# Chunk (0, 8): from reciprocals copied between partition groups by GpSimd to a VectorE mask and four identity matmuls

## The chip, the cores and the metric

One core of a Trainium2 chip runs the whole program in one launch. Five engines work side by side, each through its own queue in order: TensorE (PE in the profile, with its weight loads shown apart as PEld), VectorE (DVE), ScalarE (ACT), GpSimd (POOL) and SyncE (SP), which here only issues DMAs. The metric is the device time of the program in microseconds. Three runs of the kernel before gave a median of 184.01 us (183.97 to 184.29).

## The reference

Four batches of four heads, 1088 tokens, head dimension 32. A polynomial sketch of q and k, a linear attention over it, and then a feed-forward layer with a squared ReLU on all 4352 tokens:

```python
def phi(x):                      # x: [b, h, s, 32]; S1, S2: [8, 32]
    a = np.einsum('rd,bhsd->bhsr', S1, x)
    b = np.einsum('rd,bhsd->bhsr', S2, x)
    return np.einsum('bhsi,bhsj->bhsij', a, b).reshape(*x.shape[:-1], 64)
kv = np.einsum('bhsf,bhsd->bhfd', phi(k), v)
z = np.sum(phi(k), axis=2)
num = np.einsum('bhsf,bhfd->bhsd', phi(q), kv)
den = np.einsum('bhsf,bhf->bhs', phi(q), z)[..., None] + 1e-06
x = (num / den), heads side by side, as [4352, 128]
h = np.maximum(x @ w_in, 0.0)    # 128 -> 2048
out = h * h @ w_out              # 2048 -> 128
```

## The kernel before

**Two halves that overlap.** The attention makes `xT`, the transposed input of the feed-forward layer, in chunks. Batch 0 has three: 256 tokens made by a prologue of its own, then chunk (0, 8) and chunk (0, 20), which begin at group 8 and group 20 of 32 tokens and hold 12 and 16 groups (`nb`). The batches after have one chunk each. The feed-forward layer goes over `xT` in ten column chunks `FC` of 256, 384, 448, 448, 512, 512, 512, 512, 512 and 256 columns. Each column chunk has 16 slices of the hidden dimension, put into units of one or two slices. Per unit, TensorE runs `mm1` (line 600, into a PSUM tile `pg`), ScalarE or VectorE takes the ReLU (lines 612 and 610) and the square (lines 623 and 625), and TensorE runs `mm2` (line 644), which accumulates all 16 slices in one PSUM bank, the tile `po`. Column chunk 0 has 256 columns and units 0 to 8, so its `po` uses columns 0 to 255 of its bank. Column chunk 1 has 384 columns, units 9 to 24, and reads just the 384 tokens that chunk (0, 8) writes into `xT`.

**The steps of an attention chunk**, for chunk (0, 8), in their order:

- `qT`: VectorE transposes q; `qc` (line 306): TensorE sketches it with 32-row, 32-column tiles of its array.
- `qt` (485), `pd` (491), `rc` (501 and 505): VectorE transposes back, multiplies, sums and takes reciprocals. They stand in `rc` with a partition group (32 partitions) for each token share c and columns for each head h.
- `rl` (513): sixteen GpSimd copies, four for each c, move them to `rd`, where a partition group belongs to a head. `rl` c = 0, 1 serve the first half of the chunk, c = 2, 3 the second.
- `qb`, `qa0`, `qa1` (522), `qp` (537): six VectorE shuffles and four products make the sketch's outer products.
- `nd` (553): TensorE multiplies them with `kv`, again on 32x32 tiles, into the PSUM tile ring `att`.
- `bc` x = 0, 1 (563): VectorE broadcasts a half of `rd` along 32 columns by a transpose; `x` (570): VectorE multiplies `nd` by it and writes `xT`.

**The order of the work** is not written out. A class `_Order` is given every task with an engine, a duration, a key (its due time) and what it needs. It plays them through with durations given in the code: an engine that is free takes the ready task with the lowest key; a task that needs another engine's result is ready a `hop` of 0.25 after its end, and `lag` later still where one is given. VectorE also holds back for a task with a lower key that gets ready within half of the chosen task's duration. The instructions are then emitted in the order of the planned starts, and each engine runs its own in that order. The feed-forward matmuls have a fixed sequence among themselves; around unit 4 it is: mm2 of units 3 and 4 with mm1 of units 7 and 8 behind them, then mm2 of units 5 and 6, mm1 of unit 9, mm2 of unit 7, mm1 of unit 10. Tasks such as `qc` and `nd` are put between these as they get ready. The framework adds the semaphores between engines from the tiles that instructions read and write.

**Other names.** `iden` is the 128x128 identity, `irep` (line 730) holds a 32x32 identity in every partition group and column group, and `own_h` is [128, 4], 1 where a partition belongs to partition group h. `x0` is a PSUM tile of the prologue: TensorE writes its columns 384 to 391 (line 836), ScalarE reads these (line 840), TensorE then writes columns 256 to 383 (line 443).

Of the kernel before, what the change touches and what calls it, by code (L numbers as in the profile page):

```python
# [9 lines left out]
F32 = mybir.dt.float32  # L10
# [4 lines left out]
def _ap(t: bass.AP, p0: int, np_: int, off: int, free):  # L15
    p = list(t.ap)[0]
    return bass.AP(
        t.tensor, t.offset + p0 * p[0] + off, [[p[0], np_]] + [list(d) for d in free]
    )
# [88 lines left out]
def kernel(  # L108
# [11 lines left out]
    nc = tc.nc  # L120

    B, H, S, D = 4, 4, 1088, 32
# [6 lines left out]
    LU = 4  # L129
    KC = [(0, 160), (160, 128)]  # L130
    W0, W1, W3 = 8, 0, 1
    ND, QT, WI, KL, QL = 2, 6.0, (1.0, 1.9), (30.0, 8.0), 4.0

# [9 lines left out]
    mult = mybir.AluOpType.mult  # L145
# [8 lines left out]
    wpool = ctx.enter_context(tc.tile_pool(name="work", bufs=2))  # L154
# [5 lines left out]
    def sb(name, cols, dt=F32, rows=128):  # L160
        return cpool.tile([rows, cols], dt, tag=name, name=name)
# [90 lines left out]
    for i in range(2):  # L252
        nc.vector.memset(own_p[64 * i : 64 * i + 64, i : i + 1], 1.0)
    iden, irep = sb("iden", 128), sb("irep", 128)
# [3 lines left out]
    own_h, own_q = sb("own_h", 4), sb("own_q", 2)  # L258
# [7 lines left out]
        out=own_h[:, :], in_=_ap(iden, 0, 128, 0, [[32, 4], [1, 32]]), op=add, axis=AX  # L266
# [3 lines left out]
        out=own_f[:, :], in_=_ap(iden, 0, 128, 0, [[8, 16], [1, 8]]), op=add, axis=AX  # L270
# [6 lines left out]
    st = {}  # L277
# [4 lines left out]
    def banks(t_, x, col, n, k=2):  # L282

        return _ap(t_, 0, 128, 512 * x + col, [[512, k], [1, n]])
# [223 lines left out]
    def a_rl(b, i0, nb, c):  # L508
        n = nb // 4
        if c == 0:  # L510
            st[b, "rd", i0] = wpool.tile([128, 4 * NT], F32, tag="rd", name="rd")
        for h in range(H):
            nc.gpsimd.tensor_copy(  # L513
                st[b, "rd", i0][32 * h : 32 * h + 32, n * c : n * c + n],
                st["rc"][32 * c : 32 * c + 32, n * h : n * h + n],
            )

    def a_qs(b, i0, nb, which, x):
# [60 lines left out]
    for ci, (c0, n) in enumerate(FC):  # L579
        first_unit[c0] = len(units)  # L580
        nb = 512 // n
# [153 lines left out]
    for w in sw:  # L735
# [3 lines left out]
        out=_ap(sfk, 0, 128, 0, [[16, 2], [1, 16]]),  # L739
        in0=_ap(ss, 0, 128, 64, [[0, 2], [1, 16]]),  # L740
        in1=_ap(own_q, 0, 128, 0, [[1, 2], [0, 16]]),
        op=mult,
# [35 lines left out]
    for t0, n in ((0, 2), (2, 2), (4, 3), (7, 2)):  # L778
# [6 lines left out]
        out=_ap(qp0, 0, 128, 0, [[256, 2], [1, 256]]), in0=banks(x0, 2, 0, 256),  # L785
        in1=_ap(qb0, 0, 128, 0, [[256, 2], [1, 256]]), op=mult,
    )
    den0 = psf.tile([128, 512], F32, tag="po", name="den0")
    for y in range(2):
        nc.tensor.matmul(  # L790
            den0[64 * y : 64 * y + 64, 0:128], eps[0:1, 0:64], eps[0:1, 64:192],
            start=True, stop=False,
# [4 lines left out]
    for c in range(4):  # L797
        cast_wi(c)
    nc.vector.tensor_tensor(
        out=_ap(zb, 0, 128, 1, [[65, 2], [32, 2], [1, 1]]),  # L800
        in0=_ap(st[0, "kvp"], 0, 128, 32, [[64, 2], [0, 2], [1, 1]]),
        in1=_ap(own_p, 0, 128, 0, [[0, 2], [1, 2], [1, 1]]),
        op=mult,
    )
    nc.vector.tensor_tensor(
        out=_ap(bd, 0, 128, 0, [[64, 2], [32, 2], [1, 32]]),
        in0=_ap(st[0, "kvp"], 0, 128, 0, [[64, 2], [0, 2], [1, 32]]),
        in1=own, op=mult,
    )
    nc.vector.tensor_tensor(  # L810
        out=_ap(zm, 0, 128, 0, [[16, 2], [8, 2], [1, 8]]),
        in0=_ap(st[0, "kvp"], 0, 128, 32, [[64, 2], [0, 2], [1, 8]]),
        in1=_ap(own_f, 0, 128, 0, [[0, 2], [8, 2], [1, 8]]),
        op=mult,
# [20 lines left out]
    for h in range(H):  # L835
        nc.tensor.matmul(
            x0[32 * h : 32 * h + 32, 384:392], s2f[:, :], zm[:, 8 * h : 8 * h + 8],
            skip_group_check=True,
# [5 lines left out]
    for _ in range(W3):  # L844
# [10 lines left out]
        out=xT[:, 0:256], in0=num0[:, 0:256], in1=bc0[:, :], op=mult  # L855
# [4 lines left out]
    O = _Order()  # L860
# [11 lines left out]
    def dve(n):  # L872
        return 0.067 + n / 960
# [4 lines left out]
    def on(f, *args):  # L878
        return lambda eng: f(*args)
# [4 lines left out]
    def glued(name, dur_, to, emit, uses=[]):  # L884
        O.add(name, {"PE": dur_}, -1000.0, [to], emit, uses=uses)
        O.by_name[name]["users"] = O.by_name[to]["users"]

    def q_tasks(b, i0, nb, key):

        m = 16 * nb  # L890
        k0 = key - 6.0 - 8 * dve(m)
        names = []
        for x in range(0 if (b, i0) == (0, 8) else 2):
            i1, n1 = i0 + x * (nb // 2), nb // 2
            n1 = min(n1, G - i1)
            names.append(("qT", b, i1))
            O.add(
                names[-1], {"DVE": dve(32 * n1)}, k0 - 1.5,
                ([("qn", b)] if b else []) + prev["qTuse"], on(a_qT, b, i1, n1),
                at=QT if i0 == 20 else 0.0,  # L900
            )
        kb = KB.get((b, i0))
        O.add(
            ("qc", b, i0), {"PE": 0.75}, k0 - 1.0,
            names + [("w", b)] + ([("kT", kb, 0), ("kT", kb, 18)] if kb else []),
            on(a_qc, b, i0, nb), rings=[("att", 1)], lag=PEL, at=0.4,
        )
        if kb:
            glued(("kc", kb), 0.65, ("qc", b, i0), lambda eng: a_kc(kb, st[b, "qc", i0]))
        prev["qTuse"] = [("qc", b, i0)] if i0 + nb == 4 * NT else []  # L910
        for x in range(2):
            O.add(
                ("qt", b, i0, x), {"DVE": dve(m)}, k0 - 0.3 + 0.1 * x, [], on(a_qt, b, i0, nb, x),
                uses=[("qc", b, i0)], rings=[("qt", 1)] if x == 0 else [],
            )
        more = 0.2 if (b, i0) == (0, 8) else 0.0
        rc = [("rc", b, j) for j, _ in AC[b] if j < i0] or [("rc", b - 1, j) for j, _ in AC[b - 1]]
        O.add(
            ("pd", b, i0), {"DVE": dve(8 * nb) + more}, k0 - 0.1, rc, on(a_pd, nb),
            uses=[("qt", b, i0, 0), ("qt", b, i0, 1)],  # L920
        )
        O.add(
            ("rc", b, i0), {"DVE": 0.2 + 0.65 * more + nb * 17 / 960}, k0 - 0.1, [], on(a_rc, nb),
            uses=[("pd", b, i0)], rings=[("rc", 1)],
        )
        for c in range(4):
            O.add(
                ("rl", b, i0, c), {"POOL": 0.8 + 1.25 * more}, k0 + 0.1 * c, [], on(a_rl, b, i0, nb, c),
                uses=[("rc", b, i0)], rings=[("rd", 2)] if c == 0 else [],
            )  # L930
        for w_ in ("qb", "qa0", "qa1"):
            for x in range(2):
                O.add(
                    (w_, b, i0, x), {"DVE": dve(m)}, k0, [], on(a_qs, b, i0, nb, w_, x),
                    uses=[("qc", b, i0)], rings=[(w_, 1)] if x == 0 else [],
                )
                k0 += 0.1
        for e in range(E):
            for x in range(2):
                O.add(  # L940
                    ("qp", b, i0, e, x), {"DVE": dve(m)}, k0 + 2.0, [], on(a_qp, b, i0, nb, e, x),
                    uses=[(f"qa{e}", b, i0, x), ("qb", b, i0, x)],
                    rings=[("qp", 3), ("qp", 3)] if (e, x) == (0, 0) else [],
                )
                k0 += 0.1

    def nd_tasks(b, i0, nb, key):
        m = 16 * nb
        qps = [("qp", b, i0, e, x) for e in range(E) for x in range(2)]
        kb, vb = NK.get((b, i0)), NV.get((b, i0))  # L950

        O.add(
            ("nd", b, i0), {"PE": 0.6 + 1.05 * max(nb, 14) / 36}, key - 3.5 - 4 * dve(m),
            [("kvr", b, h) for h in range(H)]
            + ([("kT", kb, 0), ("kT", kb, 18)] if kb else [])
            + ([("vn", vb), ("ks", vb, 3)] if vb else []),
            on(a_nd, b, i0, nb, (0,) if kb or vb else (0, 1)), uses=qps + [("qp", b, i0, 0, 0)], rings=[("att", 1)], lag=PEL,
        )
        if kb:
            def behind(eng):  # L960
                a_kc(kb, st[b, "nd", i0], start=False)
                a_nd(b, i0, nb, (1,))

            glued(("kc", kb), 0.65, ("nd", b, i0), behind)
        if vb:
            def behind(eng):
                a_kvs(vb, st[b, "nd", i0], 32 * NT, start=False)
                a_nd(b, i0, nb, (1,))

            glued(  # L970
                ("kvs", vb), 1.25, ("nd", b, i0), behind, [("kp", vb, h) for h in range(H)],
            )
        for x in range(2):
            O.add(
                ("bc", b, i0, x), {"DVE": dve(m)}, key - 2.5 - 4 * dve(m) + 0.1 * x, [], on(a_bc, b, i0, nb, x),
                uses=[("rl", b, i0, 2 * x), ("rl", b, i0, 2 * x + 1)],
                rings=[("bc", 1)] if x == 0 else [],
            )
            O.add(
                ("x", b, i0, x), {"DVE": dve(m)}, key - 2.0 - 4 * dve(m) + 0.1 * x, [], on(a_x, b, i0, nb, x),  # L980
                uses=[("bc", b, i0, x), ("nd", b, i0)]
                + ([("kc", kb)] if kb else []) + ([("kvs", vb)] if vb else []),
            )
# [93 lines left out]
    for u in range(NU):  # L1077
# [40 lines left out]
        if d0 + m == NB and ci != last:  # L1118
            po = [x for u_ in range(first_unit[c0], u + 1) for x in pe2[u_]]
# [4 lines left out]
                uses=[("oT", c0)],  # L1124
# [47 lines left out]
```

## Time and profile before

| what | value |
|---|---|
| median of three runs | 184.01 us |
| time of the profiled execution | 183.99 us |
| its span (first to last instruction) | 182.1 us |
| TensorE busy | 177.3 us (97%) |
| VectorE busy | 122.1 us (67%) |
| ScalarE busy | 136.6 us (75%) |
| GpSimd busy | 39.1 us (21%) |
| granted TensorE clock | 0.998 |
| GpSimd copies of line 513, 80 in all | 19.6 us |
| of these, the 16 of chunk (0, 8) | 15.74 to 20.07 us |

The span is what the trace shows of the program's instructions; 1.9 us of the time lie outside it. Busy times overlap, so they do not add up. A matmul in float32 stands in the trace as two weight loads and two matmul records; the matmuls of `mm1`, in float32r, as one. Matmul ends are modelled and neighbours overlap in the pipeline, so the time that one costs is read from the distance to the one before it, not from its own length. The chain of waits gives this distance directly.

### The profile page before, as it was taken

The numbers are of one execution on the slowest core, as the hardware profiler recorded it, in microseconds if no ns is written. First come the engines' busy times: TensorE is split into PE (matmuls) and PEld (weight loads), VectorE is DVE, ScalarE is ACT, GpSimd is POOL, SyncE is SP. The second block draws the span as 40 slices with busy tenths as digits, with TensorE's granted clock in tenths as the row PEclk, the third lists the DMA queues.
The fourth block names the chain that finished last, engine by engine and source line by source line (L and its number), as shares of the span: only waits on it lengthen the run. The fifth ranks groups of instructions, "written<-read, shape, count | busy, mean of one in ns | idle before, by whom it ended". The sixth has DMA issues, their size and how long they took to land.

```text
span 182.1 us, 3998 instructions
## 1 busy us (share of the span) xinstructions
PE 177.3 (97%) x1530; PEld 104.6 (57%) x1530; DVE 122.1 (67%) x262; ACT 136.6 (75%) x259; POOL 39.1 (21%) x158
## 2 busy tenths in 40 slices
PE   8999999999999999999999999999999999999992
PEld 2768776656555655655555554545554555555792
DVE  5979879999999951899994335996353334333640
ACT  3449679759947886799937778995777777777980
POOL 3545318348200003470018000600000000000000
PEclk9999999999999999999999999999999999999999
DMA  5799993010029700000031200003003000300211
GB/s 174 196 274 337 246 257 96 7 29 0 0 47 243 175 0 4 4 2 0 0 54 24 34 0 5 0 0 59 0 4 58 0 0 6 51 0 0 35 26 29
DMA packets 26146, 11.26 MB, mean 62 GB/s; under 512 B 17936, under 2 KB 25104, under 8 KB 26128
## 3 DMA queue, kind: packets, MB, share of 16 engines
q1 hardware_dynamic: 25936, 10.95, 24.8%
q8 instruction: 12, 0.20, 0.4%
q10 hardware_dynamic: 192, 0.07, 0.1%
q14 instruction: 6, 0.05, 0.1%
HBM read 8.78 MB, written 2.23 MB: 60 GB/s over the span
## 4 chain that ended last, share of the span: by engine, by line
PE 93%; DMA 2%; DVE 2%; SPq 0%; issue 0%; ACT 0%; ACTq 0%
PE po L644 61%; PE pg L600 18%; PE nd L553 3%; DMA qn<-in_q_dram 2%; PE po L639 2%; PE pol L639 2%; PE qc L306 1%; PE nd L417 1%; PE kvp L399 1%; PE qc L350 1%; PE kvp L417 1%; DVE kp L334 1%; SPq L181 0%; DVE g L625 0%; PE nd L350 0%; PE den L826 0%
## 5 line engine op out<-in xcount | busy, mean ns | idle before, releaser
L644 PE MATMUL po<-g,w_o 128*128 128x512 f32 (+3 forms) x288 | 122.7, 547 | 0.2 <-DVE g L625 0.2
L612 ACT ACTIVATE gt<-pg 128x512 f32<-128x512 f32 (+3 forms) x144 | 75.3, 570 | 31.4 <-PE pg L600 30.9
L644 PEld LDWEIGHTS po<-g,w_o 128*128 128x128 f32 x288 | 53.4, 189 | 32.3 <-issue 24.6
L600 PE MATMUL pg<-xT,w_in 128*128 128x512 f32 (+3 forms) x160 | 70.2, 520 | 0.0
L623 ACT ACTIVATE g<-gt 128x512 f32<-128x512 f32 (+2 forms) x102 | 60.7, 623 | 1.6
L625 DVE TENSOR_TENSOR g<-gt 128x512 f32<-128x512 f32 (+3 forms) x43 | 30.4, 708 | 39.5 <-ACT gt L612 38.8
L600 PEld LDWEIGHTS pg<-xT,w_in 128*128 128x128 f32 x160 | 29.2, 190 | 28.3 <-ACT gt L612 11.5
L513 POOL COPY rd<-rc 32x9 f32<-32x9 f32 (+2 forms) x80 | 19.6, 246 | 25.8 <-DVE rc L505 22.6
L459 POOL COPY kv<-kvt 32x64 f32<-32x64 f32 x48 | 12.7, 265 | 44.6 <-DVE kvt L436 42.5
L522 DVE STREAM_SHUFFLE qa<-qc 128x576 f32<-128x576 f32 (+2 forms) x20 | 11.8, 648 | 0.0
L537 DVE TENSOR_TENSOR qp<-qa,qb 128x576 f32<-128x576 f32 (+2 forms) x20 | 10.8, 604 | 0.0
L485 DVE STREAM_TRANSPOSE qt<-qc 128x576 f32<-128x576 f32 (+2 forms) x10 | 5.8, 608 | 6.2 <-PE qc L350 4.5
L370 DVE TENSOR_TENSOR kp<-fs 128x576 f32<-128x576 f32 x12 | 8.7, 741 | 0.0
L648 DVE STREAM_TRANSPOSE oT<-po 128x512 f32<-128x512 f32 (+3 forms) x9 | 5.9, 654 | 2.1 <-PE po L644 2.1
L553 PE MATMUL nd<-qp,kv 32*32 32x288 f32 (+2 forms) x320 | 6.6, 354 | 0.0
L522 DVE STREAM_SHUFFLE qb<-qc 128x576 f32<-128x576 f32 (+2 forms) x10 | 6.1, 651 | 0.0
L570 DVE TENSOR_TENSOR xT<-nd,bc 128x576 fp32r<-128x576 f32 (+2 forms) x10 | 5.6, 592 | 0.5 <-PE nd L553 0.5
L299 DVE STREAM_TRANSPOSE qT<-qn 128x192 f32<-128x192 f32 (+3 forms) x11 | 5.8, 554 | 0.2 <-DMA qn<-in_q_dram 0.2
L639 PE MATMUL po<-w_o,g 128*128 128x128 f32 x32 | 5.8, 280 | 0.0
L639 PE MATMUL pol<-w_o,g 128*128 128x128 f32 x32 | 5.7, 275 | 0.0
L563 DVE STREAM_TRANSPOSE bc<-rd 128x576 f32<-128x576 f32 (+2 forms) x10 | 5.7, 598 | 0.0
L553 PEld LDWEIGHTS nd<-qp,kv 32*32 32x32 f32 x320 | 2.9, 103 | 3.6 <-issue 2.4
(106 smaller groups left out, 89.2 us busy)
## 6 DMA issues: line engine op xcount, KB each, us to landing
kn<-in_k_dram SPq DMA_DIRECT2D x3, 544.0 KB, 7.2
qn<-in_q_dram SPq DMA_DIRECT2D x3, 544.0 KB, 7.8
vn<-in_v_dram SPq DMA_DIRECT2D x9, 144.0 KB, 6.0
w_in<-in_moe_w_in_dram SPq DMA_DIRECT2D x4, 256.0 KB, 4.2
w_o<-in_moe_w_out_dram SPq DMA_DIRECT2D x4, 256.0 KB, 5.1
out_dram<-oT SPq DMA_DIRECT2D x12, 64.0 KB, 1.9
out_dram<-oT SPq DMA_DIRECT2D x8, 56.0 KB, 1.9
out_dram<-oT SPq DMA_DIRECT2D x8, 48.0 KB, 1.8
```

The lines of the kernel that those rows point to most:

```text
L370: nc.vector.tensor_tensor(out=_ap(st[b, "kp"], 0, 128, 64 * NT * h, [[64, NT], [8, 8], [1, 8]]), in0=_ap(fs, 0, 128, o, [[32, NT], [1, 8], ...
L459: nc.gpsimd.tensor_copy(_ap(st[b, "kv"], 32 * c, 32, 64 * h, [[32, E], [1, 32]]), _ap(st["kvt"], 32 * h, 32, 0, [[64, E], [1, 32]]),)
L513: nc.gpsimd.tensor_copy(st[b, "rd", i0][32 * h : 32 * h + 32, n * c : n * c + n], st["rc"][32 * c : 32 * c + 32, n * h : n * h + n],)
L522: nc.vector.stream_shuffle(in_=banks(st[b, "qc", i0], 2 * x, 0, m), out=_ap(st[b, which, i0], 0, 128, 2 * m * x, [[m, 2], [1, m]]), mask=m ...
L537: nc.vector.tensor_tensor(out=st[b, "qp", i0, e][:, r], in0=st[b, f"qa{e}", i0][:, r], in1=st[b, "qb", i0][:, r], op=mult,)
L553: nc.tensor.matmul(nd[32 * h : 32 * h + 32, 512 * c : 512 * c + m], kv[r, o : o + 32], qp[r, m * h : m * h + m], start=(e == 0), stop=(e = ...
L600: nc.tensor.matmul(st["pg", u][:, n * i : n * i + n], w_in[:, 128 * (d0 + i) : 128 * (d0 + i) + 128], xT[:, c0 : c0 + n],)
L612: nc.scalar.activation(gt[:, 0:w], st["pg", u][:, 0:w], Relu)
L623: nc.scalar.activation(to, of, Square)
L625: nc.vector.tensor_tensor(out=to, in0=of, in1=of, op=mult)
L639: nc.tensor.matmul(po[x // 128][:, 0:128], g[:, x : x + 128], w, start=(d == 0), stop=(d == NB - 1),)
L644: nc.tensor.matmul(po[0][:, 0:n], w, g, start=(d == 0), stop=(d == NB - 1))
```

## The change

For chunk (0, 8) alone, `rd` is made in another way. VectorE spreads the 12 columns of `rc` into a tile `rx` of 4 x 12 columns, each copy multiplied by one column of the mask `own_h` (task `rm`). Four float32 matmuls (task `rp`), one for each head, multiply parts of `rx` by `irep[:, 0:32]` and write 12 columns each into a partition group of `po`, columns 384 to 395 of the bank in which column chunk 0 accumulates. `bc` then reads these columns in PSUM in place of an SBUF tile. In the plan `rm` takes 0.13 of VectorE, `rp` takes 0.15 of TensorE with the key -1000 (first as soon as it is ready), and `RL` = 0.8 is its lag. The four `rl` tasks of chunk (0, 8) are left out; those of the other chunks keep their duration of 0.8.

```diff
-    ND, QT, WI, KL, QL = 2, 6.0, (1.0, 1.9), (30.0, 8.0), 4.0
+    ND, QT, WI, KL, QL, RL = 2, 6.0, (1.0, 1.9), (30.0, 8.0), 4.0, 0.8
...
+    def a_rm(nb):
+        st["rx"] = wpool.tile([128, 4 * nb], F32, tag="rx", bufs=1, name="rx")
+        nc.vector.tensor_tensor(
+            out=_ap(st["rx"], 0, 128, 0, [[nb, 4], [1, nb]]),
+            in0=_ap(st["rc"], 0, 128, 0, [[0, 4], [1, nb]]),
+            in1=_ap(own_h, 0, 128, 0, [[1, 4], [0, nb]]), op=mult,
+        )
+
+    def a_rp(b, i0, nb):
+        st[b, "rd", i0] = st["po", 0][0][:, 384 : 384 + nb]
+        for h in range(H):
+            nc.tensor.matmul(
+                st["po", 0][0][32 * h : 32 * h + 32, 384 : 384 + nb],
+                irep[:, 0:32],
+                _ap(st["rx"], 0, 128, nb // 4 * h, [[nb, 4], [1, nb // 4]]),
+                start=False, stop=True, skip_group_check=True,
+            )
...
-        for c in range(4):
-            O.add(
-                ("rl", b, i0, c), {"POOL": 0.8 + 1.25 * more}, k0 + 0.1 * c, [], on(a_rl, b, i0, nb, c),
+        if (b, i0) == (0, 8):
+            O.add(
+                ("rm", b, i0), {"DVE": 0.13}, k0 - 0.1, [], on(a_rm, nb), uses=[("rc", b, i0)],
+            )
+            O.add(
+                ("rp", b, i0), {"PE": 0.15}, -1000.0, [], on(a_rp, b, i0, nb),
+                uses=[("rm", b, i0)], lag=RL,
+            )
+        for c in range(4 if (b, i0) != (0, 8) else 0):
+            O.add(
+                ("rl", b, i0, c), {"POOL": 0.8}, k0 + 0.1 * c, [], on(a_rl, b, i0, nb, c),
                 uses=[("rc", b, i0)], rings=[("rd", 2)] if c == 0 else [],
             )
...
-                uses=[("rl", b, i0, 2 * x), ("rl", b, i0, 2 * x + 1)],
+                uses=[("rl", b, i0, 2 * x), ("rl", b, i0, 2 * x + 1), ("rp", b, i0)],
```

## The prediction

> **What bounds the kernel now.** I read first the shares of the chain of waits, from the page, then that chain in order of time around the change.
>
> ```profile
> PE 93%; DMA 2%; DVE 2%; SPq 0%; issue 0%; ACT 0%; ACTq 0%
> ```
>
> ```profile
> 16.32 0.24 PE pg L600 x2
> 16.56 0.86 PE po L644 x4
> 17.42 0.24 PE pg L600 x2
> 17.66 0.86 PE po L644 x4
> 18.52 0.23 PE pg L600 x2
> 18.76 0.89 PE nd L553 x51
> 19.65 1.92 PE po L644 x8
> 21.57 0.17 PE pg L600
> 21.74 0.86 PE po L644 x4
> 22.61 0.17 PE pg L600
> 22.78 0.43 PE qc L306 x32
> 23.21 0.71 PE qc L350 x32
> 23.92 0.37 PE pg L600
> 24.29 0.86 PE po L644 x4
> ```
>
> Columns: start, length, what. Each piece begins where the one before ends: from 13.89 on TensorE has no idle time, and the chain goes on like this to 178.87. In this stretch four records of mm2 at 256 columns take 0.86, as often as they come (0.215 each). So nothing that makes xT arrive earlier can shorten the program here, and whatever TensorE is given in addition lengthens it. That is the core of the forecast.
>
> The chain also prices a change of tile shape. Eight mm2 records should take 2 x 0.86 = 1.72; behind `nd`, on 32x32 tiles, they take 1.92. One mm1 of 384 columns takes 0.17 at 21.57 and 0.37 behind `qc` and `kc` at 23.92. So going back from small tiles to 128x128 costs 0.20, both times.
>
> Then the timeline of VectorE and GpSimd, for what the copies hold up:
>
> ```profile
> 15.74 4.33 POOL L513 COPY rd<-rc 32x3 f32<-32x3 f32 x16
> ...
> 17.19 1.15 DVE L537 TENSOR_TENSOR qp<-qa,qb 128x192 f32<-128x192 f32 x4
> 18.27 0.37 DVE L563 STREAM_TRANSPOSE bc<-rd 128x192 f32<-128x192 f32 x1
> ...
> 20.10 0.38 DVE L563 STREAM_TRANSPOSE bc<-rd 128x192 f32<-128x192 f32 x1
> 20.51 0.36 DVE L570 TENSOR_TENSOR xT<-nd,bc 128x192 fp32r<-128x192 f32 x1
> ```
>
> The copies end at 15.74 + 4.33 = 20.07, the second `bc` starts at 20.10, the second `x` ends at 20.87. That is what the copies delay. But mm1 of unit 9, which needs it, has its turn on TensorE at 21.57, 0.70 later. The copies are hidden already.
>
> **The change part by part.**
>
> *Sixteen GpSimd copies go: 4.33 of GpSimd, worth nothing.* The cover is the mm2 of units 5 and 6 (19.65 to 21.57); without it they would cost the half microsecond by which the second `x` could come earlier (right behind the first, 19.71 + 0.34, ended near 20.4).
>
> *`rm`, one VectorE product of 48 elements.* Nearest row: the product of line 810, 128x32, 0.18. I take 0.2, in front of six shuffles and four products; `qp` then ends not at 17.19 + 1.15 = 18.34 but near 18.5. `nd` waits for it, and has its turn at 18.76 before, later after the change (below). Hidden; bounds 0 and, if `nd` were up at once, 0.1.
>
> *`rp`, four matmuls, eight records, on TensorE.* The trace has the same shape once, in the prologue: 128x32 weights, four heads, eight columns.
>
> ```profile
> 10.28 0.60 PE L831 MATMUL num<-qp,bd 128*64 128x256 f32 x4
> 10.81 0.25 PE L836 MATMUL x<-zm,s2f 128*32 128x8 f32 x8
> ```
>
> The first burst ends at 10.88, the second at 11.06: 0.18, entry into the new shape included. Twelve columns in place of eight add about 0.01: 0.19. Bounds: 0.18, and 0.22 by the chain's piece for the same burst (10.88, 0.22, up to what it releases). Then the return to 128x128 weights for the second mm2 of unit 3: 0.20 (bounds: 0, if the weights are loaded meanwhile, and 0.21). Sum 0.39; between 0.18 and 0.43. I take 0.39, since the return cost stands behind `nd` and `qc` alike.
>
> The Trainium skill, TensorE: Matmul & The Clock Gate, Part 2 (step 1, LDWEIGHTS), says that TensorE pulls a weight load ahead of matmuls in flight, so that the next tile's weights load while this one runs. By that the return would be free and `rp` cost 0.19; the two returns above, 0.20 each, speak against it here. It is a rival below.
>
> *Does TensorE wait for `rp`'s input?* In the plan `rm` ends 0.13 after the reciprocal, and `rp` is ready a hop of 0.25 and `RL` = 0.8 later. Playing the code's rule on from there, the turn falls between the two mm2 of unit 3, whose four records are the 0.86 from 16.56 on: `rp` at about 16.99. The reciprocal ends at 15.61 in the trace (15.38, 0.23), `rm` near 15.8. So 1.2 to spare: no wait. If it fell short, the first to be late would be the second mm2 of unit 3, and all behind it.
>
> *`bc` reads the bank in which mm2 accumulates.* This adds a wait on both sides, and the nearest row is in the prologue: line 840 (ScalarE) reads columns 384 to 391 of `x0`, line 443 writes other columns of that bank, and it waited:
>
> ```profile
> PE x L443 <- ACT sw L840: 0.3, 1, 0.3
> ```
>
> So `bc` waits for the mm2 emitted before it, and the next mm2 waits for `bc`. Worked through, the plan takes both `bc` right behind `qp`, during the last mm2 of unit 4, ahead of mm1 of unit 8 and `nd`; mm2 of unit 5 comes behind `nd`. In the trace's times, moved by 0.39: unit 4 ends at 18.52 + 0.39 = 18.91, the two `bc` run from about 19.0 to 19.65 (0.37 each, overlapping by some 0.08 as neighbours on VectorE do), and `nd` ends at 19.65 + 0.39 = 20.04. The wait costs nothing; its cover is mm1 of unit 8 and `nd`, 1.12 together, of which 0.4 are left. On VectorE, queued behind the waiting `bc`: `qT` of the next chunk, the square of unit 7, both `x`, `kT`. Behind 19.65 come one `qT` (0.33), the square (0.65, to 20.6), both `x` (to 21.2), `kT` (1.37, to 22.5) and the other `qT` (to 22.8). TensorE needs them, at the old times and 0.39: the second `x` at 21.96, the square at 22.13, `kT` and `qT` for `qc` at 23.17. All covered, the last by 0.3 to 0.4. Reading PSUM in place of SBUF: the PSUM transposes of line 485, 128x192, took 0.63 for two, so no slower.
>
> The Trainium skill, PSUM — Partial Sum Buffer, § PSUM bank collisions raise a hardware error, tells to guard PSUM by bank and quadrant, not by address; the wait in the row above agrees. It is why the second rival below is possible at all.
>
> *Behind that.* TensorE's plan is 0.15 later throughout, and as far as I played it on (to `qc` of chunk (0, 20)) only the second `qT` of that chunk changes its place, behind `kT`. The rest should keep its order, and with TensorE never idle the 0.39 are not won back.
>
> Sum: +0.39. Own execution 183.99 to 184.38, span 182.1 to 182.5; the median of the three runs stands 0.02 higher, so 184.40 there. A measurement of this kernel can tell about 0.2% from no change, which is 0.37 us: the forecast lies on that edge.
>
> **The rivals.**
>
> 1. *The return is cheap* (the weight load hidden, as the page has it): +0.19, 184.20. For it: `rp`'s burst is only 0.06 long behind its entry, and its shape uses all rows as mm2 does. Against: both returns shown. Within 0.2%. Chance 0.10.
>
> 2. *The bank becomes a wait.* If the second `bc` is emitted behind mm2 of unit 5, as its counterpart is before the change (20.10, behind the first `x`), it must wait for that mm2 and the next must wait for it: 0.38 for `bc` and two handovers of about 0.06 (`nd` ends at 19.65, `x` starts at 19.71) are 0.5, up to 1.0 if both halves do it. With `rp`: 184.9 to 185.4. It decides from the point where the plan's VectorE reaches the second `bc` only after mm2 of unit 5 has started. Against: with the copies gone nothing else delays the second `bc`. Chance 0.14.
>
> 3. *Not slower: `rp` shares an entry and a return with another small-tile burst.* If its turn fell right ahead of `nd` (18.76), `nd` would pay for both changes of shape anyway, and `rp` cost only its stream: 11.06 - 10.81 less the first record, about 0.06: 184.07. It decides if `rp` is ready only after the last mm2 of unit 4 has begun, two mm2 tasks later than I have it. Against: in the plan's times it is ready at 4.19 and that mm2 starts at 5.74, so the lag is 1.5 short. Chance 0.06.
>
> 4. *The order behind changes after all*, keys being fixed while TensorE is later. Where it goes wrong a stall of 0.1 to 0.5 comes on top: 184.5 to 184.9. Chance 0.08. Where it goes well, one change of shape or one of the few late pieces less is won, 0.15 to 0.3, and only two or three of them together make it faster by over 0.2%: chance 0.04.
>
> That the copies do not vanish can be excluded, as no task is left that emits them.
>
> **How the numbers follow.** The forecast, +0.39 with bounds +0.18 and +0.43 and some 0.1 of scatter between runs (183.97 to 184.29), has 0.58; the rest is above. Predicted: 184.40. The range goes down to rival 3, 184.05, and up through most of rivals 2 and 4, to 184.95. Slower by over 0.2%: 0.34 of the forecast's 0.58 (its centre is just over the edge, and what is left out adds more easily than it takes away), 0.14 and 0.07: 0.55. Faster: 0.04. Same: the other 0.41.
>
> **What would show it.** Right: a burst of eight records from line `rp` between two mm2 near 17.0, 0.19 behind its neighbour, and the mm2 behind it 0.20 over its 0.215; `nd`, `qc` and everything to the end 0.39 later; both `bc` side by side during mm1 of unit 8 and `nd`; no line 513 before chunk (0, 20). Wrong: an mm2 that waits for line 563 (rival 2), idle time of TensorE before `rp` (late input), a return under 0.1 (rival 1), or a chain behind 25 whose pieces stand in another order (rival 4).

## The result and the profile after

In six runs each, taken by turns, the changed kernel had a median of 185.82 us (185.43 to 186.73) and the kernel before 184.15 us (183.97 to 184.78). The ratio of after to before is 1.0092, with a 95% interval of 1.0064 to 1.0121: slower. The forecast was 184.40 with a range to 184.95. Its direction was right, its size was not. The profiled execution of the changed kernel took 185.96, its span 184.1, at a granted TensorE clock of 1.0.

First the shares of the chain of waits, from the page of the changed kernel. Before, TensorE had 93% of the chain and SyncE's queue and the DMAs 2%.

```profile
PE 85%; SPq 7%; DMA 5%; DVE 1%; issue 1%
```

The chain now runs back from TensorE into a DMA, and 1% of it is "issue", time in which TensorE waited for nothing that the trace shows. The chain in order of time says where (start, length, what):

```profile
13.70 8.49 DMA kn<-in_k_dram
22.19 0.02 issue
22.22 1.37 DVE kT L287 x2
23.59 0.27 DVE qT L299
23.86 0.04 issue
23.90 0.50 PE qc L306 x28
24.40 0.67 PE qc L350 x32
25.07 0.37 PE pg L618
...
35.34 0.43 PE nd L571 x32
35.77 1.27 PE nd L417 x80
37.04 0.42 PE nd L571 x30
37.46 0.50 issue
37.97 0.37 PE nd L571 x2
38.34 0.84 PE po L662 x2
```

Two things are new. `qc` of chunk (0, 20), which used to start when TensorE was free for it, now follows a chain of load, `kT` and `qT`: the k of batch 1 (`kn`) lands at 22.19, and 1.37 + 0.27 of VectorE later `qc` goes on. And `nd` of chunk (0, 20) stops for 0.50 ahead of its last two records. The same place in the chain of the kernel before:

```profile
34.17 0.43 PE nd L553 x32
34.60 1.27 PE nd L417 x80
35.87 0.43 PE nd L553 x32
36.30 0.84 PE po L644 x2
```

There the 32 records of `nd`'s second half run through.

The timeline of TensorE after, around the change itself (start, length, what):

```profile
16.26 0.59 PE L662 MATMUL po<-g,w_o 128*128 128x256 f32 x2
16.79 0.25 PE L529 MATMUL po<-rx,irep 128*32 128x12 f32 x8
16.97 0.70 PE L662 MATMUL po<-g,w_o 128*128 128x256 f32 x2
...
18.93 0.96 PE L571 MATMUL nd<-qp,kv 32*32 32x96 f32 x64
```

And that of VectorE (what ended the idle time in front is in brackets):

```profile
15.40 0.43 DVE L520 TENSOR_TENSOR rx<-rc,own_h 128x48 f32<-128x48 f32 x1
...
18.80 0.65 DVE L581 STREAM_TRANSPOSE bc<-po 128x192 f32<-128x192 f32 x2 [0.23 <-PE po L662]
19.60 0.45 DVE L299 STREAM_TRANSPOSE qT<-qn 128x256 f32<-128x256 f32 x1
...
20.54 0.61 DVE L588 TENSOR_TENSOR xT<-nd,bc 128x192 fp32r<-128x192 f32 x2
22.22 1.37 DVE L287 STREAM_TRANSPOSE kT<-kn 128x576 f32<-128x576 f32 x2 [1.06 <-DMA kn<-in_k_dram]
23.51 0.34 DVE L299 STREAM_TRANSPOSE qT<-qn 128x192 f32<-128x192 f32 x1
```

In the trace of before `kT` followed the second `x` at once:

```profile
20.87 1.37 DVE L287 STREAM_TRANSPOSE kT<-kn 128x576 f32<-128x576 f32 x2
```

`rp` stands between the two mm2 of unit 3. What it costs is priced from a chain below. Both `bc` run side by side behind `qp`, waiting 0.23 for the mm2 of unit 4 ahead of them. Both `x` are done by 21.15, and then VectorE idles for 1.06, until `kn` lands. On no engine is the order of instructions different from the one worked out in the prediction.

To compare kernels I read four ends from TensorE's records in each trace: the first mm1, `nd` of chunk (0, 8), `qc` with `kc` of chunk (0, 20), and `nd` of chunk (0, 20). The distances between them, in us:

| kernel | first mm1 ends | A: to nd (0, 8) | B: to qc, kc (0, 20) | C: to nd (0, 20) | D: to the last matmul | span |
|---|---|---|---|---|---|---|
| before | 12.49 | 7.15 | 4.27 | 12.39 | 142.54 | 182.14 |
| after | 12.53 | 7.36 | 5.18 | 13.27 | 142.49 | 184.12 |
| difference | 0.04 | 0.21 | 0.91 | 0.88 | -0.05 | 1.98 |

The forecast had 0.39 in A and nothing behind it. Of A's 0.39, 0.18 is missing because the kernel before had a wait of its own there (an mm2 at 13.89 that stood 0.19 for a square), which the changed kernel's execution did not have.

### The profile page after: what moved, and what is told of

Its sections match the earlier page's. It is cut to its first block, busy times and chain, and to the rows that moved or that the text cites. A ratio compares the mean times of both kernels' runs of the same rounds, so it can differ in the third digit from the quotient of the medians.

```text
span 184.1 us, 3998 instructions
## 1 busy us (share of the span) xinstructions
PE 178.6 (97%) x1538; PEld 104.7 (57%) x1538; DVE 122.6 (67%) x263; ACT 136.7 (74%) x259; POOL 35.5 (19%) x142
## 4 chain that ended last, share of the span: by engine, by line
PE 85%; SPq 7%; DMA 5%; DVE 1%; issue 1%
PE po L662 57%; PE pg L618 17%; DMA kn<-in_k_dram 5%; PE nd L571 3%; PE po L657 2%; PE pol L657 2%; SPq L199 2%; SPq L208 2%; SPq L217 2%; PE qc L306 1%; PE nd L417 1%; SPq L187 1%; PE qc L350 1%; DVE kT L287 1%; PE kvp L417 1%
## 5 line engine op out<-in xcount | busy, mean ns | idle before, releaser
L513 POOL COPY rd<-rc 32x9 f32<-32x9 f32 (+1 forms) x64 | 16.0, 249 | 30.7 <-DVE rc L505 28.1
L581 DVE STREAM_TRANSPOSE bc<-rd 128x576 f32<-128x576 f32 (+1 forms) x8 | 4.9, 657 | 0.0
```

What stands on the lines that cost most here:

```text
L513: nc.gpsimd.tensor_copy(st[b, "rd", i0][32 * h : 32 * h + 32, n * c : n * c + n], st["rc"][32 * c : 32 * c + 32, n * h : n * h + n],)
```

## The experiments

The theory: `rp` costs about 0.4 in A; B grows when `kn` lands late, since the moved `qT` now stands behind `kT`; C grows because TensorE's stream has sixteen more instructions in front of `nd` (four float32 matmuls are eight weight loads and eight matmul records), whatever they are. Its rivals: that VectorE's new order or the shared bank makes both, or that the execution was only an unlucky one. The runs came in three groups, each on another chip; the kernels of a group ran by turns with the kernel before. Line numbers shift a little from kernel to kernel. The table has the median, the ratio to before with its interval, the fastest run less the fastest of before, and the distances in the profiled execution. `f1` to `f4` are the kernels `after_again`, `e2`, `e5` and `e6` once more, side by side in one group.

| kernel | median | ratio, interval | fastest, over before | A | B | C | D |
|---|---|---|---|---|---|---|---|
| after_again | 185.56 | 1.0088 [1.0066, 1.0109] | 1.32 | 7.36 | 4.28 | 13.25 | 142.49 |
| e1_matmuls_only | 185.03 | 1.0046 [1.0032, 1.0059] | 0.63 | 7.32 | 4.38 | 13.08 | 142.36 |
| e2_qT_first | 185.07 | 1.0054 [1.0033, 1.0074] | 1.06 | 7.43 | 4.27 | 13.42 | 142.49 |
| e3_pad | 185.80 | 1.0102 [1.0061, 1.0144] | 1.27 | 7.41 | 4.27 | 12.39 | 142.66 |
| e4_before_plus16 | 185.37 | 1.0024 [0.9996, 1.0053] | 0.59 | 6.95 | 5.15 | 13.04 | 142.34 |
| e5_after_minus16 | 185.00 | 1.0016 [0.9990, 1.0041] | 0.60 | 7.41 | 5.19 | 12.39 | 142.69 |
| e6_minus16_qT_first | 184.77 | 1.0009 [0.9976, 1.0042] | 0.42 | 7.33 | 4.28 | 12.39 | 142.82 |
| e7_with_nd | 184.58 | 0.9990 [0.9967, 1.0013] | 0.41 | 7.13 | 4.69 | 12.39 | 142.68 |
| f1_neither | 185.29 | 1.0052 [1.0032, 1.0071] | 1.34 | 7.32 | 5.06 | 13.32 | 142.47 |
| f2_qT_first | 185.05 | 1.0036 [1.0015, 1.0057] | 0.91 | 7.32 | 4.28 | 12.87 | 142.46 |
| f3_minus16 | 185.21 | 1.0049 [1.0020, 1.0079] | 0.72 | 7.33 | 5.71 | 12.39 | 142.66 |
| f4_both | 185.00 | 1.0030 [1.0000, 1.0059] | 0.41 | 7.55 | 4.28 | 12.39 | 142.55 |

The kernel before had medians of 184.04, 184.46 and 184.28 in the three groups, with fastest runs of 183.62, 183.69 and 183.63.

**after_again**: the changed kernel once more.

> The changed kernel itself once more, timed in five rounds with a second profile. Theory A (what the first profile of it shows is lasting): 185.4 to 186.2, with the kT transposes again held by the landing of kn near 22.2, qc 0.7 late on TensorE, and a gap of about 0.5 inside nd of chunk (0, 20). Theory B (both were chance in one execution, and only the matmuls last): landing near 20.9, no gap in nd, 184.3 to 184.6.

C has its 0.86 again; B has nothing this time. `kn` landed at 21.06 here, at 22.19 in the first execution. So B's 0.91 comes and goes with the execution, C's 0.88 does not.

**e1_matmuls_only**: the kernel before with its sixteen copies, plus the four matmuls on constant data (nothing reads their result; on VectorE one `bc` trades places with an `x`).

```diff
+    def a_rp(nb):
+        for h in range(H):
+            nc.tensor.matmul(
+                st["po", 0][0][32 * h : 32 * h + 32, 384 : 384 + nb],
+                irep[:, 0:32], iden[:, 0:nb],
...
+                ("rp", b, i0), {"PE": 0.15}, -1000.0, [], on(a_rp, nb),
+                uses=[("rc", b, i0)], lag=0.93,
```

> The kernel before with the four matmuls added at the same place of TensorE's stream, with the identity as their data and nobody reading the result; the GpSimd copies, bc from SBUF and the second qT ahead of kT stay as before. If TensorE's share is the forecast 0.39 and nothing else comes of these instructions: 184.4 to 184.6. If the gap in nd of chunk (0, 20) comes from where the instructions lie in TensorE's stream (sixteen more ahead of it, as in the changed kernel): the gap of 0.5 is here too, 185.0 to 185.2. If the late landing of kn comes from the added matmuls and not from the copies taken out: landing near 22.2 here too, and 0.4 more.

Neither the mask, nor a read from the bank, nor the moved `qT` is in this kernel, and yet C grows by 0.69, with a gap in the timeline of TensorE where the changed kernel has it:

```profile
36.00 0.49 PE L561 MATMUL nd<-qp,kv 32*32 32x128 f32 x30
36.83 0.37 PE L561 MATMUL nd<-qp,kv 32*32 32x128 f32 x2 [0.33 <-issue]
```

The matmuls alone bring A and C.

**e2_qT_first** and **f2_qT_first**: the changed kernel with the second `qT` of chunk (0, 20) ahead of `kT` again.

```diff
-                names[-1], {"DVE": dve(32 * n1)}, k0 - 1.5,
+                names[-1], {"DVE": dve(32 * n1)}, k0 - (5.1 if i0 == 20 else 1.5),
```

> The changed kernel with the second qT of chunk (0, 20) back ahead of kT on VectorE (its key lowered), all other queues unchanged. If qc waits for the chain landing of kn, kT, qT: 0.27 less than the changed kernel in the same call (the qT's pitch in its profile). If the landing is early enough in most executions: no difference, under 0.1.

> Second corner: the second qT ahead of kT, the gap left. Theory: 0.9 to 1.1 over before (0.39 + about 0.65), gap in nd. If only the qT's place matters and the gap is the profiler's: 0.4.

B is 4.27 and 4.28, and C keeps its excess (13.42 and 12.87). The chain of e2 in order of time has 0.67 of "issue" in `nd`, and its `qc` and `kc` run without a stop:

```profile
23.17 0.43 PE qc L306 x32
23.60 0.71 PE qc L350 x32
...
36.27 0.42 PE nd L571 x30
36.70 0.67 issue
37.36 0.37 PE nd L571 x2
```

So the two losses are separate. In e2 `kn` landed at 21.67, 0.2 later than the changed kernel could have borne without loss (see below), in f2 at 20.94.

**e3_pad**: the changed kernel with sixteen tiny matmuls more (32 instructions) in the prologue, behind a warm-up burst.

```diff
     keep_warm(W0)
+    for _ in range(16):
+        nc.tensor.matmul(
+            st["warm"][0:32, 0:8],
+            nc.const_aps.tensor(1.0, (128, 32), mybir.dt.bfloat16),
+            nc.const_aps.tensor(1.0, (128, 8), mybir.dt.bfloat16),
+        )
```

> The changed kernel with 32 more TensorE instructions (16 matmuls of 128x32 weights and 8 columns) in the idle time of the prologue before 4.2 us, so that all later instructions lie 32 further in TensorE's stream. If the gap in nd of chunk (0, 20) comes from a boundary in the stream of instructions: it moves to 32 instructions earlier, into the 80 matmuls of kvs or the nd before, and stays about as long; with the first matmuls of the prologue not late, the time is that of the changed kernel or up to 0.5 less. If it is a wait for data: it stays at the same matmul.

With 48 instructions ahead in place of 16 the gap is gone: C is 12.39 to the hundredth, as before the change, and the chain shows the second half of `nd` in one piece.

```profile
38.05 0.43 PE nd L571 x32
```

Neither expectation had this: the gap neither moved 32 instructions ahead nor stayed. The total is no better, though, as TensorE's prologue ran 1.9 later by the first mm1 (14.41 against 12.49). The added matmuls take some 0.5 of that (the burst of line 318 begins at 5.65, in the other traces at 4.89 to 5.18); the rest came of bursts that ran slower, which f4 has without any added matmuls (see the last section). Its time says nothing of the gap; the distance C does.

**e4_before_plus16**: the kernel before, nothing of the change, with one prologue step cut into four 32-column matmuls in place of two of 64 for each of two blocks: sixteen instructions more.

```diff
-    a_kf(7, 2, psf, "pg", 64)
+    a_kf(7, 2, psf, "pg")
```

> The kernel before with sixteen more TensorE instructions in the prologue (the last keys' sketch in 32-column instead of 64-column pieces: four more float32 matmuls, each two weight loads and two matmuls); all behind it unchanged, just sixteen instructions further in TensorE's stream. Theory P (the gap in nd of chunk (0, 20) comes from where the instructions lie): the gap of 0.5 to 0.8 is there though none of the change is, and the time is 184.5 to 184.8. Theory Q (the gap comes from the added burst itself or from TensorE being 0.39 later): no gap, 184.0 to 184.1.

The gap is there, without any part of the change behind the prologue:

```profile
36.80 0.42 PE nd L553 x30
37.23 0.29 issue
37.52 0.38 PE nd L553 x2
```

C is 13.04. A is 6.95, the least of all: without `rp` and without the wait at 13.89. Its B is long for another reason, the q of batch 1, which landed at 19.87 and made `qT`, a square, both `x` and then an mm1 late. Its median, 0.91 over before, lies above both forecasts, and the interval of its ratio still holds 1: that the gap is there is shown by the trace, not by the time.

**e5_after_minus16** and **f3_minus16**: the changed kernel with another prologue step of two blocks in 64-column matmuls, sixteen instructions fewer, so that the stream behind `rp` stands where it stood before.

```diff
-    a_kf(2, 2, psf, "pg")
+    a_kf(2, 2, psf, "pg", 64)
```

> The changed kernel with sixteen instructions fewer in the prologue (the second keys' sketch in 64-column pieces), so that all behind the four added matmuls lies as in the kernel before. Theory P: no gap in nd of chunk (0, 20), 0.65 less than the changed kernel (185.56 in the first call), 184.8 to 185.1. Theory Q: gap and time as in the changed kernel, 185.4 to 185.7.

> Third corner: sixteen instructions fewer in the prologue, the qT left behind kT. Theory: 0.7 to 1.0 over before (0.39 and 0.3 to 0.6 for the qT's place, by where kn lands), no gap. If the gap does not exist without the profiler: as the changed kernel, 1.4 to 1.7.

C is 12.39 in both. B is 5.19 and 5.71: here `kn` landed at 22.16 and 23.14, and the chain of e5 shows the same links as that of the changed kernel.

```profile
13.66 8.50 DMA kn<-in_k_dram
22.16 0.02 issue
22.19 1.37 DVE kT L287 x2
23.56 0.27 DVE qT L299
23.83 0.04 issue
23.87 0.50 PE qc L306 x28
...
37.01 0.43 PE nd L571 x32
```

Landing and links add up to the end of `kc`: 0.02 + 1.37 + 0.27 + 0.04 + 0.50 + 0.67 = 2.87. By that the four executions with a late `kn` should end it at 25.06 (after), 25.28 (f1), 25.03 (e5) and 26.01 (f3); they ended it at 25.07, 25.29, 25.04 and 26.02.

**e6_minus16_qT_first** and **f4_both**: both edits together.

> Both mended in the changed kernel: sixteen instructions fewer in the prologue, and the second qT of chunk (0, 20) ahead of kT as before. If the loss has just three parts (matmuls 0.39, gap 0.65, the qT's place 0.3 to 0.5), only the matmuls are left: 184.3 to 184.6. If something else of the change costs (bc from the accumulating bank, the missing copies): over 184.8.

> Fourth corner: both. Theory: 0.3 to 0.5 over before, the matmuls alone. If the parts do not add up: over 0.7.

B is 4.28 and C 12.39 in both. What is left of the change is `rp`; the chain of f4 prices it:

```profile
18.80 0.43 PE po L662 x2
19.23 0.18 PE po L529 x8
19.41 0.63 PE po L662 x2
```

Two mm2 records ahead of `rp` take 0.43, two behind it 0.63: 0.18 for `rp`, 0.20 for the return. The medians, 0.31 and 0.72 over before, are too wide apart to price 0.38, and 0.72 is over the 0.7 that the expectation of f4 set for parts that do not add up; the fastest runs, 0.42 and 0.41 over before, agree with 0.38. f4's profiled execution was one with a slow prologue (first mm1 at 14.72).

**e7_with_nd**: e5's prologue, the second `qT` ahead of `kT` as before, and `rp` emitted right ahead of `nd`, into `nd`'s PSUM tile, so that both share the change of shape (rival 3 of the prediction). `bc` reads there, behind `nd`.

```diff
             st[b, "nd", i0] = att("nd")
+            if (b, i0) == (0, 8):
+                a_rp(b, i0, nb)
...
-                st["po", 0][0][32 * h : 32 * h + 32, 384 : 384 + nb],
+                st[b, "nd", i0][32 * h : 32 * h + 32, 384 : 384 + nb],
```

> As e6, with the four matmuls moved right ahead of nd and written into nd's own PSUM tile, so that bc waits for nd and no longer for the bank of mm2; all orders but these as in the kernel before. The going back to 128x128 weights is then paid by nd alone: the matmuls should cost their entry and stream, 0.12 + 0.06, in place of 0.39: 184.15 to 184.3. If the return cost of 0.20 is not what the 0.39 holds: 184.4 or more.

```profile
18.72 0.25 PE L529 MATMUL nd<-rx,irep 128*32 128x12 f32 x8
18.91 0.96 PE L573 MATMUL nd<-qp,kv 32*32 32x96 f32 x64
...
21.96 0.41 PE L620 MATMUL pg<-xT,w_in 128*128 128x384 f32 x1 [0.17 <-DVE xT L590]
```

`rp` costs its 0.19 and no return of its own, `nd` begins as late behind it as behind an mm1: A is 7.13, that is 0.18 over e4's 6.95. The 0.06 that rival 3 priced is not reached. The mm1 that reads the first `x` now waits, with both `bc` behind `nd` and a q that landed at 19.45. Its median is the lowest of the versions with the change, and its interval does not tell it from the kernel before.

**f1_neither**: the changed kernel a third time.

> The four corners in one call, so that they share the chip and the runs of before: this is the changed kernel as it is. If the gap and the qT's place each cost what the profiles show, 1.4 to 1.7 over before; gap in nd in its profile.

B 5.06 (`kn` at 22.41), C 13.32. In three executions the excess in C was 0.88, 0.86 and 0.93. The median is 1.01 over before, less than the 1.4 expected.

**What each part is worth.** The gap in C is in every kernel with sixteen more instructions (seven executions, 12.87 to 13.42) and in none with as many as before or 48 more (seven, 12.39 each). A late start does not make it: the first mm1 of f2 ended 1.2 later than that of before and the gap is there, that of f4 2.2 later and there is none. A little of it comes back in D, which is 142.34 to 142.49 in the executions with the gap and 142.54 to 142.82 in the others; no run tells why.

In time the parts are less clear. The kernels with the place of `qT` put back are faster than their counterparts in the same group by 0.49, 0.24, 0.23 and 0.21 (medians: e2, f2, e6, f4): four times the same way, but in each pair the runs of the two kernels overlap. In the four corners, taking the gap away gained next to nothing by the medians (f1 less f3 0.08, f2 less f4 0.05). Seven of the 24 runs of f3 and f4 are over 186 us and one of the 24 of f1 and f2; of those profiled, f4's (186.62) had the slow prologue and f3's (186.22) the late loads. The edit that takes the gap away also lengthens the burst of line 318, from 1.37 in before to 1.67 in e5. So what the gap costs in a middling run is not shown.

The fastest runs, which late landings and slow prologues touch least, add up: 0.41 for `rp` (e6, f4), 0.2 to 0.3 for the place of `qT` (e5 and f3 less that), 0.5 to 0.65 for the gap (e2 and f2 less that), together 1.1 to 1.4; 1.32 and 1.34 were measured for all three (after_again, f1). e1, with `rp` and the gap, does not fit by its fastest run (0.63), only by its median (0.99). The fastest of before comes from 17 or 35 runs and those of the others from 6 or 12, so each of the single figures may be high by some tenth.

## Why the prediction was wrong

*`rp` costs 0.39* held: 0.18 for its stream with the entry, 0.20 for the return, and A, in the eleven executions with `rp` in that place, is 0.37 to 0.41 over e4's 6.95, once the idle time of TensorE in it (up to 0.09, in f4 0.19) is taken off. *Copies worth nothing, `rm` hidden, input in time, `bc`'s wait covered* held too. `rx` took 0.43 in place of the 0.2 estimated and `bc` waited 0.23, and no matmul was late for either.

*Rival 1, the return is cheap*, fell at 0.20. By the Trainium skill, TensorE: Matmul & The Clock Gate, Part 2 (step 1), a weight load is pulled ahead of matmuls in flight if their row groups do not conflict or if it goes to the background weight buffer, so the weights behind `rp` could have been loaded while it runs. The trace does not show that for this change of tile shape: the weight load behind `rp` begins at 16.96, when the burst is all but over (17.04), and behind `nd` and `qc` 0.20 is paid as well. Which of the two conditions was not met, no run tells. *Rival 2, the bank becomes a wait*: no mm2 waited for line 581. *Rival 4*: the order behind is the one forecast.

Two steps failed.

*"All covered, the last by 0.3 to 0.4."* This let `kT` begin as soon as VectorE was free and asked only whether VectorE reached `qT` in time. `kT` waits for the load of `kn` as well. In the trace of before, that load landed at 20.84 and `kT` began at 20.87, right behind the second `x`: no wait to be seen, so I took none. But the load had just made it. In the thirteen other executions, none of whose edits touches it, it landed between 20.72 and 23.14. With `qc` due at 23.17 as forecast, the changed kernel has slack for a landing up to 23.17 - 1.37 - 0.27 - 0.04 - 0.02 = 21.47, the kernel before up to 22.78 - 1.37 - 0.04 - 0.02 = 21.35. A later `kn` delays either; the moved `qT` adds its 0.27 to the changed kernel alone, while `rp`'s 0.39 costs nothing more where TensorE would wait for the load anyway. So with `kn` at 22.19 the kernel before would have had `qc` at 23.62 (22.19 + 1.43), the changed one had it at 23.90. By this working 0.28 of the delay of `qc` belongs to the change in that pair of traces, and the rest to the execution. It is worked out, not shown: only one trace of the kernel before was taken, and its load was early.

*"The rest should keep its order, and with TensorE never idle the 0.39 are not won back."* The order was kept, and still TensorE became idle in C: for 0.12 to 0.67 in the seven traces with the gap, which with the two records behind it made C 0.48 to 1.03 longer. The step took it that work inserted into a full engine costs its own time and nothing else. Sixteen instructions more in front also moved what comes later to another place in TensorE's stream, and there `nd`'s dense run of small matmuls stops once. By the traces and the fastest runs this is the largest part of the miss, and it has nothing to do with reciprocals: e4 has it too.

In sum: forecast 0.39; `rp` is 0.38 of it, the gap some 0.6 in the fastest runs (0.86 to 0.93 in the three traces), the place of `qT` 0 to 0.27 depending on the load. The rest of the 1.67 between the two medians of the result is not accounted for; late loads delay either kernel. The chance of slower had been put at 0.55; the range ended at 184.95, under the fastest run of the changed kernel in the result (185.43), because no rival had a price for a stall that no wait explains or for a load that lands at another time.

What makes the gap is open. The trace has a clue: rows of 16 KB instruction fetches on one queue. The fetch near `nd` of chunk (0, 20), read from the trace's DMA packets:

```
kernel   nd begins   fetch begins   nd's gap
before     34.10        35.33        none
e3         36.28        34.12        none
e6         34.59        35.94        none
after      35.27        35.33        37.46 to 37.97
e2         34.50        34.59        36.70 to 37.36
e4         35.03        35.25        37.23 to 37.52
```

Where the fetch begins along with `nd` there is a gap about two us later; where it begins over a microsecond into `nd`, or two ahead of it, there is none. The other eight traces do the same: the fetch begins 0.06 to 0.21 behind `nd` in the four with a gap and 1.31 to 1.70 behind it in the four without. One reading is that a block of instructions comes too late for so dense a burst. No run changed the fetch itself, so this is not shown.

## What to carry to other kernels

A step that begins exactly when its input lands has no slack that the trace can show: before anything is put behind such a step, look for a load among its inputs and ask how far its landing scatters. Small instructions inserted into a saturated engine cost here their time, the change of shape, and the place of everything behind them; a gap marked "issue" in a burst that was whole before is a case for shifting the stream by a few instructions, with nothing else changed, before the edit is blamed. And small-tile work belongs next to other small-tile work: beside `nd` the same four matmuls cost 0.18 of TensorE in place of 0.38.

## What was not expected of the hardware

The landing of one 544 KB load, issued at 13.2 to 13.9 in all executions, scattered by 2.4 us with the DMA engines full (share 1.0 in this stretch). The gap in `nd` went with the number of TensorE instructions in front, whatever these were: with 16 more it was 0.48 to 1.03 in C, with 48 more or as many as before 0.00.

And TensorE's prologue has slow executions. The trace's record of the granted clock begins with an entry at full clock: at 4.06 in before, at 9.20 in e3, at 10.09 in f4. Ahead of this entry no clock is recorded, and the rows of the profile, which show 1.00 there, say nothing of it. Bursts ahead of the entry ran slower: the sixteen matmul records of `x` from `qT` (line 757 in before) took 1.16 in e3 and f4, where they lie ahead of it, and 0.69 in the twelve other traces, where they lie behind it. The burst of line 318, with 64 records in both, took 1.37 in before and 2.35 in e3. All that follows starts up to 2.2 us later. So it looks as if the full clock came late in these executions; no run here tells why. The late start of f2 is another matter: there the burst of line 399 stood 1.18 for a load of v.
